# Moving two pieces of routing work on VectorE: a comparison of the third round behind two row residuals, and the one-hots of two experts ahead of the next update

## The chip, the cores and the metric

The kernel runs on one core of a Trainium2 chip. The metric is device time in microseconds (us) of one execution, as the median over executions. Engines are named as the profile names them: PE (TensorE matmul), PEld (TensorE weight load), DVE (VectorE), ACT (ScalarE), POOL (GpSimd) and SP (SyncE, which issues DMAs). POOL issues DMAs as well, the gathers and scatters by index among them.

## The reference, cut to what matters

A gated linear attention over 3072 tokens is followed by a mixture of eight experts with a hard capacity. Which expert a token gets depends on a greedy walk over all (token, expert) logits in descending order.

```python
# attention: state = alpha*state + k v^T ; y = q . state, per head -> x of shape (3072, 384)
logits = x @ w_gate                       # 3072 x 8
order = np.argsort(-logits.flatten())
for idx in order:
    tok, e = idx // E, idx % E
    if assigned[tok] >= 0 or counts[e] >= cap: continue   # cap = 384
    assigned[tok] = e; counts[e] += 1
for e in range(E):
    mask = assigned == e
    h = np.maximum(x[mask] @ w1[e], 0.0)  # 384 x 1024
    out[mask] = h @ w2[e]                 # 384 x 384
```

## The kernel before

**Two phases.** The first 135 us or so are the attention. Its engine orders come from a planner in the kernel (`Plan`), and the change doesn't touch it. The second phase routes and runs the experts, one after the other. Its order is made when the program is built. The framework takes the program order as a priority and its own estimate of durations, and fixes one order per engine, which the chip then keeps. A block under `tc.high_priority()` ranks ahead. `tc.issue_after(x)` adds an edge: the instructions of the block stand behind `x` in the order of the engine that both run on. The block waits for nothing that its data doesn't need, apart from its place in the line.

**Rounds.** Experts are handled in the order in which they fill up, so round i finds the i-th expert to be closed (i runs from 0 to 7; the third round is i = 2). Each round has these steps, all mostly on DVE with small matmuls on PE between them:

- `search(i)` (L712 on): five or six levels. A level compares a digit of each token's key with a ramp (`compare`, output `cmp`, L683), counts by matmul (`rt`, L745, L748 or L751), subtracts and compares (`need` L757 or L762, `gt` L764), sums by one matmul (L772), reduces (`k`, L776) and forms the next digit (`nd`, L779). Its end yields the expert's number (`ei`), and `weights` loads that expert's w1 and w2 in halves through SP.
- `extract(i)` (L914 on): turns the chosen tokens' ranks into a list of row numbers. It writes one-hots (`hot` L931, `rhs` L934), multiplies them on PE (`xt` L944), adds four small pieces into `idx` (L955, L956), and POOL then gathers three blocks of 128 rows of x (`xr`, L963).
- `update(i)` (L842 on): takes the closed expert out and makes the keys of round i + 1, with the first-level comparison of that round (`cmp` on a digit `dig`) in it. In the program it stands in the loop of round i + 1, ahead of `search(i + 1)`.

In rounds 0 to 2 the variable `st["hot"]` holds the last instruction of the one-hots of `extract` (the product `rhs` in rounds 1 and 2), and the next `update` is placed behind it with `issue_after`. For later rounds there is no such edge, and `update` goes where the framework puts it.

**The expert itself.** `prep(i)` (L1032 on) transposes the three gathered blocks on PE (L1046), ACT copies each as `xh` (L1049), and DVE takes the row residual `xl = xt - xh` (L1051, `XD` in the changed kernel). The transposes for expert i stand behind the matmuls of block 5 of the expert before. Then come eight blocks of `ffn1` (L1062; `hh` on ACT L1066, `hl` on DVE L1067) and `ffn2` (`y`, L1082). Every product is done as three matmuls with high and low parts. `split` makes these parts of the weights: ACT copies `w1hi`, `w1lo`, `w2hi`, `w2lo` (L1005), and a POOL DMA then adds the raw weight onto the negative copy (`w1lo`, `w2lo`, L993).

The transposes and the one-hot product share two PSUM banks (`psx`), so block 2 of the rows can be transposed only when `xl` of block 0 has been read from its bank.

The line that places the second-level comparison (`t == 1`) puts it behind the newest `idx`:

```python
            with tc.issue_after(st["idx"].ins) if i and t == 1 else ExitStack():
                nc.vector.tensor_tensor(words(dst, nt, js), keyed(d, nt, js), each(iotas[t], nt, js), op=OP.is_ge)
```

Of the kernel before, what the change touches and what calls it, by code (L numbers as in the profile page):

```python
# [157 lines left out]
def gla_moe_kernel(ctx, tc, q, k, v, alpha, w_gate, w1, w2, out):  # L158
    nc = tc.nc
# [66 lines left out]
    def each(table, n, js):  # L226
        return table[:, None, :n].to_broadcast([128, (js.stop - js.start) // U, n, U])

    def keyed(x, n, js):
        return x[:, js].rearrange("p (w u) -> p w u", u=U)[:, :, None, :].to_broadcast(  # L230
            [128, (js.stop - js.start) // U, n, U])

    def words(x, n, js):
        return x[:, js.start // U:js.stop // U, :n]
# [61 lines left out]
    def levels(i):  # L296
        return BITS if i < LATER else LATER_BITS
# [344 lines left out]
    def row(x, w=NU):  # L642
        return x[:, :, None].to_broadcast([128, NU, w])
# [32 lines left out]
    def compare(i, d, t):  # L676
        nt = 2 ** levels(i)[t]
        dst = cbuf[t % 2]
        if nt < T:
            dst = dst.rearrange("p w (h t) u -> p (w h) t u", h=T // nt)  # L680
        for js in halves(i, 2 * nt == T, 0 if t else 3):
            with tc.issue_after(st["idx"].ins) if i and t == 1 else ExitStack():
                nc.vector.tensor_tensor(words(dst, nt, js), keyed(d, nt, js), each(iotas[t], nt, js), op=OP.is_ge)  # L683
            yield dst, js

    def halves(i, pairs, parts=0):
        if i == 1 and not pairs and parts:
            return [slice(a, a + NU // parts) for a in range(0, NU, NU // parts)]
        if i:
            return [slice(0, NU)]  # L690
        return [slice(0, 16), slice(16, NU)] if pairs else [slice(0, NU // 2), slice(NU // 2, NU)]
# [4 lines left out]
    def pair(x, j):  # L696
        return x.rearrange("p w t u -> p (w t u)")[:, 64 * U * (j // U) + j % U:64 * U * (j // U + 2):U]

    st = dict(chu=chu0, o=o0, dig=dig0)

    def spin_after(n, *after):
        if n:
            o = fps.tile([128, CAP], F32, name="h", bufs=2)
            with ExitStack() as es_:
                for x in after:
                    es_.enter_context(tc.issue_after(x.ins))
                for _ in range(n):
                    x = nc.tensor.matmul(o, warm[:, :128], warm[:, :CAP], start=True, stop=True)
            after = [x]
        return after  # L710

    def search(i):  # L712
# [12 lines left out]
        for t, bits in enumerate(levels(i)):  # L725
# [3 lines left out]
            else:  # L729
                g = (gs if i < LATER else later_gs[bits])[t % 2]  # L730
                parts = compare(i, d, t) if t else [(cbuf[0], js) for js in halves(i, False)]
                rt = fps.tile([128, 64], F32, name="rt")
                two, four = 2 * nt == T, 4 * nt == T
# [180 lines left out]
    def extract(i):  # L914
        vi = rw.tile([128, NU], I16, name="vi")
        if st["v1"] is None:
            nc.vector.tensor_scalar(vi, st["v"], -1.0, None, op0=OP.add)
        else:
            nc.vector.scalar_tensor_tensor(vi, st["v"], -1.0, st["v1"], op0=OP.add, op1=OP.add)
        wi = rw.tile([128, NU], I16, name="wi")  # L920
        nc.vector.tensor_scalar(wi, vi, 63, None, op0=OP.bitwise_and)
        bi = rw.tile([128, NU], I16, name="bi")
        nc.vector.tensor_scalar(bi, vi, 32704, None, op0=OP.bitwise_and)
        bk = rw.tile([128, NU, 2 * NB], F16, name="bk")
        x = nc.vector.tensor_tensor(bk, row(bi, 2 * NB), bsel, op=OP.is_equal)
        hot = rw.tile([128, NW, 64, U], F16, name="hot", bufs=1)
        rhs = rw.tile([128, NU, 2 * NB], F16, name="rhs")
        alone = i == 0
        for a, js in enumerate(halves(i, True)):
            with tc.issue_after(x.ins):  # L930
                x = nc.vector.tensor_tensor(words(hot, 64, js), keyed(wi, 64, js), each(iota_0, 64, js), op=OP.is_equal)  # L931
            if a == 0:
                with tc.issue_after(x.ins):
                    y = nc.vector.tensor_tensor(rhs, bk, cst, op=OP.mult)  # L934
                x = y
        if i < 3:
            st["hot"] = x
        ix = psx.tile([128, 2, 2, NB], F32, name="xt")
        with ExitStack() as es_:
            if i == 0:  # L940
                for x in st["spin"]:
                    es_.enter_context(tc.issue_after(x.ins))
            for j in [j for j in range(NU) if j // U % 2 == 0]:
                st["picked"] = nc.tensor.matmul(ix, pair(hot, j), rhs[:, j:j + U + 1:U],  # L944
                                                start=(j == 0), stop=(j == NU - U - 1))
        IDX[i] = rw.tile([128, NB], I32, name="idx", bufs=4)
        lo, hi = slice(0, 64), slice(64, 128)
        other = rw.tile([128, NB], F32, name="other")
        if alone:
            nc.scalar.activation(other[hi], ix[lo, 0, 1], AF.Copy)  # L950
            nc.vector.tensor_copy(other[lo], ix[hi, 1, 0])
        else:
            nc.vector.tensor_copy(other[lo], ix[hi, 1, 0])
            nc.vector.tensor_copy(other[hi], ix[lo, 0, 1])
        nc.vector.scalar_tensor_tensor(IDX[i][lo], ix[lo, 0, 0], float(N // 2), other[lo], op0=OP.add, op1=OP.add)  # L955
        st["idx"] = nc.vector.scalar_tensor_tensor(IDX[i][hi], ix[hi, 1, 1], float(N // 2), other[hi],  # L956
                                                   op0=OP.add, op1=OP.add)
        if i == 0:
            st["spin"] = spin_after(WARM_IN_ROUTE[0], st["picked"])
        if i:  # L960
            XR[i] = wp.tile([128, NB, Dm], F32, name="xr")
        for b in range(NB):
            gathers[b] = last_gather[0] = nc.gpsimd.indirect_dma_start(  # L963
                out=XR[i][:, b], out_offset=None, in_=x_dram,
                in_offset=bass.IndirectOffsetOnAxis(ap=IDX[i][:, b:b + 1], axis=0))

        for load_, b in second_half:
            tc.add_manual_dep(load_(1).ins, gathers[b].ins.name,
                              mybir.DependencyInfo(mybir.DependencyClass.Sync, mybir.DependencyReason.DATA),
                              reason="rows of the first experts before their later weights")  # L970
        second_half.clear()

    last_gather, gathers = [None], {}

    XH, XL, CH, XA = {}, {}, {}, {}

    def split(i, hf):
        fs = slice(hf * F // 2, (hf + 1) * F // 2)
# [53 lines left out]
    def prep(i):  # L1032
        hi = wp.tile([128, DB, CAP], F32R, name="xh")
        lo = fp.tile([128, DB, CAP], F32R, name="xl")
        for b in range(NB):
            bs = slice(b * 128, (b + 1) * 128)
            o = psx.tile([128, DB, 128], F32, name="xt")
            with ExitStack() as es:
                if i:
                    es.enter_context(tc.issue_after(F2[i - 1, FB - 3].ins))  # L1040
                else:
                    st["spin"] = spin_after(WARM_IN_ROUTE[1 + b], *st["spin"])
                    for x in st["spin"]:
                        es.enter_context(tc.issue_after(x.ins))
                for d in range(DB):
                    x = nc.tensor.transpose(o[:, d], XR[i][:, b, d * 128:(d + 1) * 128], ident)  # L1046
                if i == 0:
                    st["spin"] = [x]
            XA[i] = nc.scalar.activation(hi[:, :, bs], o, AF.Copy)  # L1049
            with tc.high_priority():  # L1050
                nc.vector.tensor_sub(lo[:, :, bs], o, hi[:, :, bs])  # L1051
        XH[i], XL[i] = hi, lo

    HH, HA, F1, HL = {}, {}, {}, {}
# [47 lines left out]
    for n in range(E * FB + 2):  # L1102
        i, q = divmod(n, FB)
# [17 lines left out]
        if n >= 2:  # L1121
            i, q = divmod(n - 2, FB)
# [53 lines left out]
```

## Time and profile before

| | |
|---|---|
| median of 3 executions | 416.37 us (413.94, 416.37, 419.88) |
| the profiled execution's own time | 413.29 us |
| its span, from the first to the last instruction | 411.6 us |
| PE busy over the span | 385.0 us (94%) |
| PEld busy | 340.6 us (83%) |
| DVE busy | 283.3 us (69%) |
| ACT busy | 214.5 us (52%) |
| POOL busy | 186.8 us (45%) |
| mean granted TensorE clock | 0.991 |

The profile is of one execution. A row of the order of time gives the start in us, the duration in us, the engine, the line of the kernel, the operation, what it writes and reads with the shapes, and in square brackets how long the engine had been idle just before and what ended that idle time. Durations overlap a little with the next row on the same engine, so the spacing of starts is the better measure of what one instruction costs. Everything between the last instruction and the end of the execution (413.29 less 411.6, 1.69 us) lies outside the span.

### The profile page before, as it was taken

Reading aid. Unit: us, or ns where it says so; the run is one execution under the profiler, and the core shown is the slowest. Engines: PE = TensorE matmul, PEld = TensorE weight load, DVE = VectorE, ACT = ScalarE, POOL = GpSimd, SP = SyncE. Lnnn points to the kernel's source line nnn. Section 1 sums busy time; section 2 is a strip of 40 time slices with the busy share of each in tenths; the row PEclk is TensorE's granted clock in tenths of the full one; section 3 lists DMA queues with packets and bytes.
Section 4 is the critical chain, followed back from the end, with each engine's and each line's share of the span. In section 5 each row is a group of like instructions: output and inputs, shape, how many; then the busy total and the mean of one; then the engine's idle time right before and its main releaser. Section 6 shows DMA issues by size and latency. Waiting matters only on the chain.

```text
span 411.6 us, 9897 instructions
## 1 busy us (share of the span) xinstructions
PE 385.0 (94%) x3775; PEld 340.6 (83%) x3775; DVE 283.3 (69%) x909; ACT 214.5 (52%) x382; POOL 186.8 (45%) x230
## 2 busy tenths in 40 slices
PE   6899999999999888898999998999999999999992
PEld 3788889887888556797798997899998999999992
DVE  8889997899994686687586796597796872312210
ACT  3456555654553015626639629529529539478211
POOL 5899988566851016213405506216126263614102
PEclk9899999999999999999999999999999999999998
DMA  8989898763020148789799999979999999999601
GB/s 274 378 284 309 276 311 230 245 200 105 22 79 30 50 151 204 164 204 262 206 220 323 200 282 274 213 252 278 210 298 226 197 303 327 247 305 202 155 0 58
DMA packets 43711, 88.05 MB, mean 214 GB/s; under 512 B 3856, under 2 KB 18192, under 8 KB 43664
## 3 DMA queue, kind: packets, MB, share of 16 engines
q0 software_dynamic: 11408, 33.83, 38.9%
q1 hardware_dynamic: 32256, 53.60, 38.5%
q8 instruction: 29, 0.48, 0.5%
q14 instruction: 18, 0.15, 0.1%
HBM read 53.59 MB, written 9.44 MB: 153 GB/s over the span
## 4 chain that ended last, share of the span: by engine, by line
PE 48%; DVE 16%; issue 15%; DMA 14%; POOL 3%; ACT 1%; POOLq 0%; SPq 0%; DVEq 0%
PE h L1062 12%; PE y L1082 11%; DMA w1r<-in_moe_w_dram 4%; PE xt L421 4%; PE y L484 4%; DMA w1lo<-w1r 4%; PE y L477 4%; PE s L433 4%; DMA xr<-x_dram,idx 3%; DMA w2lo<-w2r 3%; DVE te L393 3%; PE lg L502 2%; DVE tp L399 2%; PE rt L751 1%; PE st L445 1%
## 5 line engine op out<-in xcount | busy, mean ns | idle before, releaser
L1066 ACT ACTIVATE hh<-h 128x384 fp32r<-128x384 f32 x64 | 31.3, 488 | 85.3 <-PE h L1062 62.5
L1067 DVE SCALAR_TENSOR_TENSOR hl<-h,hh 128x384 fp32r<-128x384 f32 x64 | 35.4, 553 | 51.0 <-ACT hh L1066 50.7
L1082 PE MATMUL y<-w2hi,hh 128*128 128x384 f32 x192 | 66.6, 347 | 0.0
L1082 PE MATMUL y<-w2lo,hh 128*128 128x384 f32 x192 | 65.8, 343 | 0.4 <-DMA w2lo<-w2r 0.4
L1082 PE MATMUL y<-w2hi,hl 128*128 128x384 f32 x192 | 65.3, 342 | 0.0
L1094 POOL DMA_INDIRECT out_dram<-yt,idx x24 | 25.5, 1062 | 50.5 <-ACT yt L1087 46.8
L1062 PE MATMUL h<-xh,w1lo 128*128 128x384 f32 x192 | 46.9, 343 | 0.0
L1062 PE MATMUL h<-xh,w1hi 128*128 128x384 f32 x192 | 46.0, 342 | 0.6 <-ACT xh L1049 0.6
L1062 PE MATMUL h<-xl,w1hi 128*128 128x384 f32 x192 | 45.8, 342 | 0.0
L993 POOL DMA_DIRECT2D w1lo<-w1r x15 | 20.3, 1350 | 55.7 <-ACT w1lo L1005 40.1
L963 POOL DMA_INDIRECT xr<-x_dram,idx x24 | 26.2, 1092 | 40.4 <-DVE idx L956 26.2
L1062 PEld LDWEIGHTS h<-xh,w1hi 128*128 128x128 f32 x192 | 33.9, 188 | 4.4 <-issue 2.9
L403 POOL TENSOR_TENSOR kh<-rk,te 128x512 f32<-128x512 f32 (+1 forms) x24 | 29.4, 1226 | 17.1 <-DVE z L413 11.4
L1082 PEld LDWEIGHTS y<-w2lo,hh 128*128 128x128 f32 x192 | 36.3, 189 | 0.7 <-DMA w2lo<-w2r 0.7
L1082 PEld LDWEIGHTS y<-w2hi,hh 128*128 128x128 f32 x192 | 36.3, 189 | 0.0
L1082 PEld LDWEIGHTS y<-w2hi,hl 128*128 128x128 f32 x192 | 36.2, 189 | 0.1
L1062 PEld LDWEIGHTS h<-xl,w1hi 128*128 128x128 f32 x192 | 33.8, 189 | 0.5 <-DVE xl L1051 0.2
L1062 PEld LDWEIGHTS h<-xh,w1lo 128*128 128x128 f32 x192 | 33.9, 189 | 0.4 <-DMA w1lo<-w1r 0.3
L1005 ACT ACTIVATE w1hi<-w1r 128x768 fp32r<-128x768 f32 x32 | 26.8, 840 | 10.4 <-DMA w1r<-in_moe_w_dram 8.0
L435 ACT ACTIVATE sm<-s 128x1024 f32<-128x1024 f32 x24 | 24.6, 1026 | 13.9 <-PE s L433 13.4
L399 DVE TENSOR_TENSOR_SCAN tp<-al,z 128x512 f32<-128x512 f32 (+1 forms) x26 | 29.6, 1138 | 2.6 <-DVE z L413 0.5
L393 DVE TENSOR_TENSOR_SCAN te<-al,z 128x511 f32<-128x511 f32 (+2 forms) x26 | 30.8, 1186 | 0.5
(204 smaller groups left out, 833.8 us busy)
## 6 DMA issues: line engine op xcount, KB each, us to landing
w1r<-in_moe_w_dram SPq DMA_DIRECT2D x16, 768.0 KB, 7.7
w2r<-in_moe_w_dram SPq DMA_DIRECT2D x16, 768.0 KB, 10.0
w2lo<-w2r POOLq DMA_DIRECT2D x16, 768.0 KB, 10.4
w1lo<-w1r POOLq DMA_DIRECT2D x15, 768.0 KB, 8.0
al<-in_alpha_dram SPq DMA_DIRECT2D x24, 260.0 KB, 4.1
rk<-in_k_dram SPq DMA_DIRECT2D x24, 256.0 KB, 4.2
rq<-in_q_dram SPq DMA_DIRECT2D x24, 256.0 KB, 4.4
rv<-in_v_dram SPq DMA_DIRECT2D x24, 192.0 KB, 3.9
```

The costliest lines, as they stand in the source:

```text
L393: nc.vector.tensor_tensor_scan(te.t[:, lo:top][:, ::-1], al.t[:, lo + 1:top + 1][:, ::-1], zb[:, lo + 1:top + 1][:, ::-1], al.t[:, 4 * C + ...
L399: nc.vector.tensor_tensor_scan(tp.t[:, lo:hi], al.t[:, lo:hi], zb[:, lo:hi], 1.0, op0=OP.mult, op1=OP.add)
L403: eng.tensor_tensor(out_.t[:, us].rearrange("p u c -> p (u c)"), x.t[:, lo:hi], f.t[:, lo:hi], op=OP.mult)
L435: add(A_, 1.05, lambda: nc.scalar.activation(sm.t, sc.t, AF.Copy), r=[(sc, 0), (sc, 1)], w=[sm])
L963: gathers[b] = last_gather[0] = nc.gpsimd.indirect_dma_start(out=XR[i][:, b], out_offset=None, in_=x_dram, in_offset=bass.IndirectOffsetOn ...
L993: return nc.gpsimd.dma_start(x.bitcast(F32), raw_, accum_op=OP.add, max_dma_last_dim=8192)
L1005: nc.scalar.activation(dst, src, AF.Copy, scale=scale)
L1062: F1[i, q] = nc.tensor.matmul(o, a[:, d], x[:, d], start=(n == 0), stop=(n == 3 * DB - 1))
L1066: HA[i, q] = nc.scalar.activation(hh, o, AF.Relu)
L1067: HL[i, q] = nc.vector.scalar_tensor_tensor(hl, o, 0.0, hh, op0=OP.max, op1=OP.subtract)
L1082: F2[i, q] = nc.tensor.matmul(Y[b], a[:, bs], w, start=(q == 0 and n == 0), stop=(q == FB - 1 and n == 2))
L1094: st_ = nc.gpsimd.indirect_dma_start(out=out, out_offset=bass.IndirectOffsetOnAxis(ap=IDX[i][:, b:b + 1], axis=0), in_=yt, in_offset=None)
```

## The change

Two orders on DVE are written anew; no instruction is added or taken out.

1. In round 2 the second-level comparison stands behind `XD[1, 1]`, the row residual of the second block of expert 1 (and so behind that of the first block too), where it stood behind `idx` of round 1. All other rounds keep their place for it.
2. `st["hot"]` is kept for rounds 0 to 4, where it was kept for rounds 0 to 2. So `update(3)` and `update(4)` stand behind the one-hots of `extract(3)` and `extract(4)`, the fourth and fifth expert.

```diff
@@ compare
-            with tc.issue_after(st["idx"].ins) if i and t == 1 else ExitStack():
+            behind = XD[1, 1] if i == 2 else st.get("idx")
+            with tc.issue_after(behind.ins) if i and t == 1 else ExitStack():
@@ extract
-        if i < 3:
+        if i < 5:
             st["hot"] = x
@@
-    XH, XL, CH, XA = {}, {}, {}, {}
+    XH, XL, CH, XA, XD = {}, {}, {}, {}, {}
@@ prep
             with tc.high_priority():
-                nc.vector.tensor_sub(lo[:, :, bs], o, hi[:, :, bs])
+                XD[i, b] = nc.vector.tensor_sub(lo[:, :, bs], o, hi[:, :, bs])
```

## The prediction, made before the changed kernel ran

> **What bounds the kernel now.** First the page's head, then busy time in stretches of the expert phase, then PE's waits from 180 us to the end.
>
> ```profile
> span 411.6 us, 9897 instructions
> PE 385.0 (94%) x3775; PEld 340.6 (83%) x3775; DVE 283.3 (69%) x909; ACT 214.5 (52%) x382; POOL 186.8 (45%) x230
> 176.00:210.00 34.00, 31.60 (x257) 28.44 (x256) 24.35 (x90) 18.07 (x30) 10.73 (x10) 1.00 0.91 225
> 210.00:240.00 30.00, 29.12 (x224) 26.88 (x223) 23.13 (x95) 18.14 (x30) 11.30 (x10) 1.00 1.04 255
> 240.00:262.00 22.00, 19.94 (x157) 17.76 (x156) 15.83 (x64) 14.79 (x24) 7.61 (x7) 1.00 1.02 270
> 262.00:300.00 38.00, 37.98 (x287) 34.61 (x286) 29.62 (x128) 21.22 (x37) 13.13 (x14) 1.00 0.98 239
> 300.00:340.00 40.00, 40.00 (x295) 37.09 (x294) 30.94 (x134) 21.93 (x36) 16.61 (x14) 1.00 0.99 260
> ```
>
> The stretch rows give the stretch, its length, then busy time of PE, PEld, DVE, ACT and POOL, the granted clock, the DMA share and GB/s. From 262 us on PE is never free (37.98 of 38, 40.00 of 40), at a clock of 1.00. So PE's work sets the end, and what the change can take out is PE's idle time ahead of 262 us: 34.00 - 31.60 = 2.40, then 0.88, then 2.06, together 5.34 us. Both edits act after 190 us. PE's waits say who caused it (total, times, longest; the first two):
>
> ```profile
> PE xt L1046 <- DMA xr<-x_dram,idx: 3.0, 2, 1.6
> PE rt L772 <- DVE gt L764: 1.3, 2, 0.9
> ...
> ```
>
> More than half is waiting for gathered rows. One of these two waits (3.0 - 1.6 = 1.4 us, expert 1) lies ahead of both edits. The other is expert 3's, and the order of time shows it with the rest of what can move:
>
> ```profile
> 196.99 0.98 PE L1062 MATMUL h<-xh,w1hi 128*128 128x384 f32 x4 [0.57 <-ACT xh L1049]
> ...
> 201.66 0.44 PE L1082 MATMUL y<-w2lo,hh 128*128 128x384 f32 x1 [0.42 <-DMA w2lo<-w2r]
> ...
> 221.11 0.17 PE L772 MATMUL rt<-gt,one 128*128 128x8 bf16 x1 [0.88 <-DVE gt L764]
> ...
> 252.65 0.17 PE L772 MATMUL rt<-gt,one 128*128 128x8 bf16 x1 [0.42 <-DVE gt L764]
> ...
> 257.90 1.02 PE L1046 MATMUL xt<-ident,xr 128*128 128x128 f32 x6 [1.64 <-DMA xr<-x_dram,idx]
> ```
>
> **The change, edit 2 first (one-hots of experts 3 and 4 ahead of the update).** DVE and POOL in round 3:
>
> ```profile
> 241.02 0.25 DVE L837 SCALAR_TENSOR_TENSOR v<-cum,rt,qe 128x24 f32<-128x24 f32 x1
> ...
> 244.03 0.95 DVE L683 TENSOR_TENSOR cmp<-dig,iota 128x1536 bf16<-128x1536 bf16 x1
> ...
> 246.68 0.94 DVE L931 TENSOR_TENSOR hot<-wi,iota 128x1536 f16<-128x1536 int16 x1
> ...
> 249.26 0.17 DVE L956 SCALAR_TENSOR_TENSOR idx<-xt,other 64x3 int32<-64x3 f32 x1
> 249.46 0.96 DVE L683 TENSOR_TENSOR cmp<-nd,iota 128x1536 bf16<-128x1536 bf16 x1
> ...
> 249.34 1.33 POOL L993 DMA_DIRECT2D w1lo<-w1r  x1 [13.84 <-ACT w1lo L1005]
> 250.98 1.07 POOL L963 DMA_INDIRECT xr<-x_dram,idx  x1 [0.30 <-issue]
> ```
>
> The whole update ran between v and hot, and on POOL a w1lo DMA stood in front, so the gather began 250.98 - 241.02 = 10.0 us after v. Rounds 1 and 2 already have the new order:
>
> ```profile
> 179.22 0.25 DVE L837 SCALAR_TENSOR_TENSOR v<-cum,rt,qe 128x24 f32<-128x24 f32 x1 [0.30 <-PE rt L830]
> ...
> 183.13 1.09 POOL L963 DMA_INDIRECT xr<-x_dram,idx  x1 [8.11 <-DVE idx L956]
> ...
> 211.12 0.25 DVE L837 SCALAR_TENSOR_TENSOR v<-cum,rt,qe 128x24 f32<-128x24 f32 x1
> ...
> 217.73 1.65 POOL L963 DMA_INDIRECT xr<-x_dram,idx  x1 [10.34 <-DVE idx L956]
> ```
>
> There the gather began 3.9 and 6.6 us after v. Expert 3's will therefore begin between 241.02 + 3.9 = 244.9 and 241.02 + 6.6 = 247.6, ahead of the w1lo DMA of 249.34, which is 3.4 to 6.1 us earlier than before. The rows should arrive as much earlier, and the 1.64 us wait goes even at the lesser end. What stands late next is PE itself: the transposes keep their place behind block 5 of expert 2, whose matmuls ended at 257.90 - 1.64 = 256.26. **Term A: -1.64 us.** For expert 4 the same is worth nothing on PE, because 262 to 300 has no idle time; PE's own work hides it.
>
> The price of edit 2 is that update(3) and update(4), and with each the first comparison of the next round, start later by the extract instructions put ahead:
>
> ```profile
> 213.64 0.16 DVE L844 SCALAR_TENSOR_TENSOR pen<-cl,pen 128x8 f32<-128x8 f32 x1
> ...
> 221.80 0.96 DVE L683 TENSOR_TENSOR cmp<-nd,iota 128x1536 bf16<-128x1536 bf16 x1
> ...
> 224.74 0.56 DVE L683 TENSOR_TENSOR cmp<-nd,iota 128x768 bf16<-128x768 bf16 x1
> ```
>
> In round 2, 213.64 - 211.12 = 2.52 us passed from v to pen, the update's first instruction. An hl between them (0.47 by spacing, as xl of the same size below) and the two v (0.25 to 0.5) come off: 1.7 us. So the first comparison of round 4 moves from 244.03 to about 245.7. Before, 5.43 us passed from it to the second one (249.46), because that stood behind idx and the extract instructions sat between its steps. A level without them takes 224.74 - 221.80 = 2.94 us. With the four pieces of idx (0.2 each, by 249.26 to 249.46) and an hl (0.47) it is 4.2, and the second comparison comes at 249.9 against 249.46; without these it would be 248.6. I take 0 for the later rounds, between -0.8 and +0.4; if the planned order leaves the steps as far apart as they are, it is +1.7.
>
> **Edit 1 (the comparison of round 2 behind two residuals).**
>
> ```profile
> 191.94 0.49 ACT L1049 ACTIVATE xh<-xt 128x384 fp32r<-128x384 f32 x1 [0.66 <-PE xt L1046]
> ...
> 192.99 1.76 DVE L683 TENSOR_TENSOR cmp<-nd,iota 128x3072 bf16<-128x3072 bf16 x1
> 194.66 1.01 DVE L1051 TENSOR_TENSOR xl<-xt,xh 128x384 fp32r<-128x384 f32 x2
> ...
> 196.97 0.56 DVE L1051 TENSOR_TENSOR xl<-xt,xh 128x384 fp32r<-128x384 f32 x1 [0.32 <-ACT xh L1049]
> 197.44 0.23 DVE L779 SCALAR_TENSOR_TENSOR nd<-nd,k,dig 128x24 bf16<-128x24 bf16 x1
> ```
>
> Both inputs of the two residuals were there at 192.43, but they waited for a comparison of 1.7 us, and block 2's transposes, xh and the first matmul of expert 1 waited with them. Turned round, the residuals end about 1.7 us earlier, and the comparison starts 1.0 us later (two residuals), or 0.5 if the first of them fits into the wait for k. Queued behind the comparison are that level's count, k and nd, and then all of round 2 up to the weights of expert 2. In return the third residual (0.47 us, with 0.32 of waiting) no longer stands in front of the next nd, which gives 0.8 back: the search comes out between -0.3 and +0.2. On PE the 0.57 at 196.99 can go, but PE then meets the w2lo DMA earlier, which ends at 201.6 whatever DVE does, so its 0.42 grows to 1.0. **Term B: 0**, between -0.6 (if PE has other work for that wait) and +1.0 (if nothing is given back: weights of expert 2 later, ACT's copies later, and the 0.88 at 221.11 longer). The 0.42 at 252.65 lies in DVE's reordered stretch and can go or double; I take 0 and keep both ends.
>
> Sum: 413.29 - 1.64 = 411.65 us for an execution like the profiled one (span 411.6 - 1.64 = 409.96; the 1.69 us outside it stay). That execution was faster than all three timed ones, so on the median 416.37 - 1.64 = **414.7 us**, with -0.6 to -2.6 of change (413.8 to 415.8) as this case's own range.
>
> **Rivals.** *The earlier gather takes its time from the weights.* The four weight halves of expert 3 are in flight then:
>
> ```profile
> 240.67 0.38 SPq L658 DMA_DIRECT2D w1r<-in_moe_w_dram  x1
> ...
> GB/s 221 180 229 179 229 125 305 317 384 368 399 405 399 394 380 379 352 164 172 188 183 188 120 219 349 378 211 242 188 213 188 191 205 199 202 240 188 248 188 205
> ...
> 251.65 0.56 DVE L1067 SCALAR_TENSOR_TENSOR hl<-h,hh 128x384 fp32r<-128x384 f32 x1 [1.23 <-ACT hh L1066]
> ...
> 252.25 0.83 ACT L1005 ACTIVATE w1hi<-w1r 128x768 fp32r<-128x768 f32 x1
> ```
>
> The second row cuts 238 to 268 us into 40 slices. While the loads ran alone they moved 380 to 405 GB/s (about 245 to 250 us). The gather's three blocks (3 x 128 x 384 x 4 bytes, 0.59 MB) are 1.5 us at 394 GB/s. ACT copies these weights, and hh stands between the copies: hl waited 1.23 us for it, and the 0.42 at 252.65 is gt behind that hl. Loads 1.5 us late would cost PE 1.5 there: -1.64 + 1.5, **416.2 us**. [...] The trace of before has no gather beside loads at full rate, so it can't settle this. Against it: the copy of the second half of w1 began at 252.25 without a wait, so ACT was behind the loads already.
>
> *The pushed updates carry through (the other side).* If the 1.7 us of rounds 4 and 5 stay, the weights of experts 4 and 5 come 1.7 and 3.4 us later, while PE is 1.64 earlier. Their slack shows in the landing of the first w2lo:
>
> ```profile
> 285.02 1.03 POOL L993 DMA_DIRECT2D w2lo<-w2r  x1
> ...
> w2lo<-w2r POOLq DMA_DIRECT2D x1, 768.0 KB, 9.1
> ...
> 295.83 0.34 PE L1082 MATMUL y<-w2lo,hh 128*128 128x384 f32 x1
> ```
>
> Issued at 285.02, it landed at 294.1, 1.7 us before its use. It decides from a delay of 0.1 us on, once PE is 1.64 earlier: expert 4 gives back 1.6, expert 5 another 1.7. Net -1.64 + 3.3 = +1.7: **418.1 us**. Against it: expert 4's w2lo stood behind its gathers on POOL, and these come earlier too.
>
> *The waits of DVE's order go as well.* If also 0.57, 0.42 and the 0.88 of 221.11 vanish, it is -1.64 - 1.87 = -3.5: **412.9 us**. For it speaks that a DVE order caused them; against it the w2lo landing.
>
> *The order doesn't change.* Excluded: cmp at 192.99 precedes xl at 194.66, and the update's comparison at 244.03 precedes hot at 246.68.
>
> **How the numbers follow.** Chances: forecast 0.50, gather against weights 0.20, pushed updates 0.15, more waits gone 0.12, others 0.03. The range must hold all but the outermost: from 412.9 less 1.1 to the 418.1 of the slower rival, the more so because the three executions of before differ by 6 us: 411.8 to 418.2. About 2% is what a measurement of this kernel tells from no change, and that is 8.3 us. Even all 5.34 us of idle time are less, so faster by 2% gets 0.02; slower by 2% gets 0.03, for an order that leaves PE without work in several rounds; within 2% gets 0.95.
>
> **What would show it.** In the changed profile: idx of round 3 before 247.5 and its gather ahead of the w1lo DMA; no PE wait for xr at expert 3, and PE at its transposes at 256.3; the second comparison of round 4 at 249 to 250; in round 2 xl, xl, then cmp, with PE's wait for w2lo near 1.0 and none for xh. The forecast is wrong if PE's wait turns up at 252 (weights), at the first w2lo of experts 4 and 5 (updates), or grows beyond 0.88 at 221.

## The result, and the profile after

The change made the kernel slower by 0.8%: 418.60 us (median of 20 executions) against 415.46 us (20), ratio 1.0077 with a 95% interval of 1.0048 to 1.0107. The forecast was 414.7 us, within 411.8 to 418.2. The sign was wrong, and the median lies just above the range. The forecast stood on the 416.37 of three executions; from 415.46 the same sum gives 413.8. All ratios here and below are of the fast executions alone, those within 1.5% of their kernel's fastest, so they are not the quotients of the medians beside them.

The profiled execution of the changed kernel took 420.92 us. Line numbers stand one higher than before from `compare` on. First the head of its page:

```profile
span 418.9 us, 9895 instructions
...
PE 390.0 (93%) x3775; PEld 344.6 (82%) x3775; DVE 285.2 (68%) x909; ACT 214.3 (51%) x382; POOL 187.2 (45%) x230
```

Then its busy time in the stretches shown of before (PE, PEld, DVE, ACT, POOL, clock, DMA share, GB/s):

```profile
176.00:210.00 34.00, 32.58 (x264) 29.29 (x263) 23.51 (x81) 17.35 (x29) 11.93 (x11) 0.95 0.87 218
210.00:240.00 30.00, 29.47 (x224) 26.98 (x224) 22.39 (x93) 18.64 (x31) 11.36 (x10) 1.00 1.03 252
240.00:262.00 22.00, 18.20 (x141) 16.61 (x141) 14.62 (x64) 10.79 (x17) 6.04 (x5) 1.00 0.96 262
262.00:300.00 38.00, 38.00 (x279) 34.73 (x278) 27.70 (x113) 24.12 (x40) 15.23 (x14) 0.96 0.87 213
300.00:340.00 40.00, 38.37 (x282) 35.11 (x282) 31.35 (x142) 20.18 (x34) 11.80 (x11) 1.00 1.01 244
```

Up to 240 us PE did lose less: 34.00 - 32.58 = 1.42 and 0.53 us idle, against 2.40 and 0.88. Then it lost more: 3.80 us against 2.06 between 240 and 262, and 1.63 against 0.00 between 300 and 340. PE's instructions also took longer, 390.0 us against 385.0 for the same 3775, and the clock says why (0.95 and 0.96 in two stretches, and a fall ahead of them, below). PE's waits from 176 us on, in order of time:

```profile
191.64 0.55 PE L1047 MATMUL xt<-ident,xr 128*128 128x128 f32 x3 [1.38 <-DMA xr<-x_dram,idx]
222.47 0.17 PE L773 MATMUL rt<-gt,one 128*128 128x8 bf16 x1 [0.39 <-DVE gt L765]
260.65 0.55 PE L1047 MATMUL xt<-ident,xr 128*128 128x128 f32 x3 [3.67 <-DMA xr<-x_dram,idx]
319.12 0.17 PE L773 MATMUL rt<-gt,one 128*128 128x8 bf16 x1 [1.41 <-DVE gt L765]
...
370.21 0.81 PE L1063 MATMUL h<-xh,w1lo 128*128 128x384 f32 x3 [0.67 <-DMA w1lo<-w1r]
```

The 0.57, 0.42 and 0.42 of before are gone and the 0.88 is 0.39. The wait for expert 3's rows, which the forecast took away, has grown from 1.64 to 3.67 us. DVE and POOL in round 3 show why the rows weren't earlier:

```profile
243.68 0.25 DVE L838 SCALAR_TENSOR_TENSOR v<-cum,rt,qe 128x24 f32<-128x24 f32 x1 [0.20 <-PE rt L831]
...
245.18 0.95 DVE L932 TENSOR_TENSOR hot<-wi,iota 128x1536 f16<-128x1536 int16 x1
...
249.39 0.96 DVE L684 TENSOR_TENSOR cmp<-dig,iota 128x1536 bf16<-128x1536 bf16 x1
...
250.71 0.16 DVE L957 SCALAR_TENSOR_TENSOR idx<-xt,other 64x3 int32<-64x3 f32 x1
253.59 0.96 DVE L684 TENSOR_TENSOR cmp<-nd,iota 128x1536 bf16<-128x1536 bf16 x1
...
252.12 1.34 POOL L994 DMA_DIRECT2D w1lo<-w1r  x1 [15.40 <-ACT w1lo L1006]
253.75 1.74 POOL L964 DMA_INDIRECT xr<-x_dram,idx  x1 [0.30 <-DVE nd L780]
```

The one-hots do stand ahead of the update now, and `idx` ended 250.87 - 243.68 = 7.2 us after v instead of 8.4. But POOL still had the `w1lo` DMA in front of the gather, and that DMA waits for ACT's copies. So the gather began 2.9 us after `idx` was done, and 253.75 - 243.68 = 10.07 us after v, against 9.96 before. PE, relieved of small waits, came to its transposes 260.65 - 3.67 - 243.68 = 13.30 us after v, against 256.26 - 241.02 = 15.24 before. The arithmetic closes: 1.64 + (15.24 - 13.30) + (10.07 - 9.96) = 3.69. **Counted from v, all that PE had saved was handed back at this wait**, because the gather's time behind v didn't move with it.

Two things came on top. First, the clock behind the long wait, in the changed kernel:

```profile
262.00:265.00 3.00, 3.00 (x14) 2.60 (x12) 1.30 (x5) 2.45 (x4) 1.31 (x1) 0.53 0.66 133
265.00:268.00 3.00, 3.00 (x24) 2.83 (x22) 2.07 (x8) 1.98 (x4) 1.05 (x1) 0.91 0.93 161
```

PE was busy all the time and got 0.53 and 0.91 of its clock: 3 x 0.47 + 3 x 0.09 = 1.7 us lost. Before, behind a wait of 1.64, it was 1.00. Second, the 1.41 at 319.12, which ACT and DVE explain:

```profile
313.93 0.84 ACT L1006 ACTIVATE w1hi<-w1r 128x768 fp32r<-128x768 f32 x1 [3.36 <-DMA w1r<-in_moe_w_dram]
...
317.62 0.47 ACT L1067 ACTIVATE hh<-h 128x384 fp32r<-128x384 f32 x1
318.12 0.56 DVE L1068 SCALAR_TENSOR_TENSOR hl<-h,hh 128x384 fp32r<-128x384 f32 x1 [1.88 <-ACT hh L1067]
318.91 0.16 DVE L765 TENSOR_TENSOR gt<-rt,need 64x8 bf16<-64x8 f32 x1
```

ACT stood 3.36 us for a weight load, with five copies ahead of `hh` in its queue. DVE's `hl` waited for `hh`, and the search's `gt` stood behind `hl`.

From 176 us on PE idled 7.74 us, the rows above and one of 0.22, against 5.29 before: +2.45, and 1.7 by the clock at 262 to 268. The two profiled executions differ by 7.6 us, the medians by 3.1. So this execution also holds losses that others don't. The clock fell twice ahead of all this: to 0.76 and 0.67 in the 3 us from 165 and from 168, and to 0.81 and 0.62 in those from 192 and from 195, where the kernel before had 1.00. That is 3 x (0.24 + 0.33 + 0.19 + 0.38) = 3.4 us, the larger part of PE's 5.0. The waits in front (1.29 us at 165.17, 1.38 at 191.64) come ahead of both edits, and e20 below, which has neither edit, shows 0.86 and 0.57, and 0.91 and 0.52, in the same stretches. So these 3.4 us are not the edits'.

### The profile page after: what moved, and what is told of

The parts are those of the page before. It is cut to its first block, busy times and chain, and to the rows that moved or that the text cites. A ratio compares the mean times of both kernels' runs of the same rounds, so it can differ in the third digit from the quotient of the medians.

```text
span 418.9 us, 9895 instructions
## 1 busy us (share of the span) xinstructions
PE 390.0 (93%) x3775; PEld 344.6 (82%) x3775; DVE 285.2 (68%) x909; ACT 214.3 (51%) x382; POOL 187.2 (45%) x230
## 4 chain that ended last, share of the span: by engine, by line
PE 45%; issue 18%; DVE 16%; DMA 14%; POOL 4%; ACT 2%; POOLq 0%; DVEq 0%; SPq 0%; ACTq 0%
PE y L1083 10%; PE h L1063 9%; DMA xr<-x_dram,idx 5%; PE xt L421 4%; DMA w1lo<-w1r 4%; PE y L484 4%; PE s L433 4%; PE y L477 4%; DMA w1r<-in_moe_w_dram 3%; DVE te L393 3%; PE lg L502 2%; DVE tp L399 2%; DMA out_dram<-yt,idx 2%; PE xt L1047 2%; PE h L709 2%
## 5 line engine op out<-in xcount | busy, mean ns | idle before, releaser
L1083 PE MATMUL y<-w2hi,hh 128*128 128x384 f32 x192 | 67.7, 353 | 0.0
L1083 PE MATMUL y<-w2lo,hh 128*128 128x384 f32 x192 | 67.3, 351 | 0.0
L1083 PE MATMUL y<-w2hi,hl 128*128 128x384 f32 x192 | 66.3, 347 | 0.0
```

Source lines behind the costliest of these rows:

```text
L1083: F2[i, q] = nc.tensor.matmul(Y[b], a[:, bs], w, start=(q == 0 and n == 0), stop=(q == FB - 1 and n == 2))
```

## The experiments

Theory 1: the gather behind `w1lo` on POOL makes the loss. Theory 2: the pushed updates of rounds 4 and 5 make it. Theory 3: the longer wait's clock. All ratios are against executions of the kernel before that were timed with the run, with a 95% interval. The median of these was 414.4 to 415.5, so ratios are better compared than medians.

**Each edit alone.** e1 keeps edit 1 only:

```diff
-        if i < 5:
+        if i < 3:
             st["hot"] = x
```

> Edit 1 alone (comparison of round 2 behind the residuals; the one-hots of experts 3 and 4 as before). Theory A (the later comparison delays rounds 2 and 3, and with them the weights and the gather of expert 3, which stands behind the w1lo DMA on POOL): PE's wait for xr at expert 3 is above 2.5 us, and the time is 1.5 to 3.5 us above the kernel before. Theory B (the pushed updates of rounds 3 and 4 are to blame): the wait stays near 1.6 us or below, and the time is within 1 us of before or less. Theory C (no order is to blame, the changed kernel's orders only fall worse with the transfers of expert 0): within 1 us of before.

Measured: 416.56 us, 1.0062 (1.0023 to 1.0102). PE and POOL of e1 in order of time:

```profile
256.95 1.02 PE L1047 MATMUL xt<-ident,xr 128*128 128x128 f32 x6 [2.96 <-DMA xr<-x_dram,idx]
...
248.40 1.34 POOL L994 DMA_DIRECT2D w1lo<-w1r  x1 [14.85 <-PE xt L945]
250.04 1.07 POOL L964 DMA_INDIRECT xr<-x_dram,idx  x1 [0.30 <-DVE cmp L684]
```

Its busy time and clock just behind the wait:

```profile
259.00:262.00 3.00, 3.00 (x19) 2.60 (x19) 0.89 (x2) 2.19 (x4) 1.30 (x1) 0.51 0.60 114
```

Edit 1 does speed PE up: its idle time from 176 to 240 is 1.39 us in e1, 3.23 before. PE came to the transposes at 253.99, found no rows, waited 2.96, and got half its clock for 3 us. It waited another 1.44 us for the rows of expert 4, at 291.06. The saving turned into longer waits, and the clock's 1.5 us added to the loss. The expectation of e1 had put such a wait down to later routing, but v of round 3 came 240.49 - 190.40 = 50.09 us after expert 1's transposes began, and 241.02 - 190.20 = 50.82 before. PE was early, and the routing wasn't late.

e2 keeps edit 2 only (`compare` as before); e3 and e4 take it apart by expert:

```diff
-        if i < 3:
+        if i < 4:             # e3: expert 3 alone
+        if i < 3 or i == 4:   # e4: expert 4 alone
             st["hot"] = x
```

> Edit 2 alone, both experts. Theory A: within 1 us of the kernel before, with PE's wait for xr at expert 3 at 0.5 to 2 us. Theory B: 2 to 4 us slower, with a new wait at expert 4 or 5 (around 319 us in the changed kernel, 1.4 us, for gt). Theory C: within 1 us. The prediction on record would have 1.6 us faster, with no wait for xr at expert 3.

> Edit 2 for expert 3 alone (update(3) behind its one-hots, update(4) as before, edit 1 left out). Theory A: within 1 us of before. Theory B: if the push of round 4 is the loss, 1 to 2 us slower; if it is that of round 5, none. On POOL the gather of expert 3 stands behind the w1lo DMA as before, so it begins no more than 1 us earlier than 250.98, and PE's wait for xr stays between 0.6 and 1.7 us.

> Edit 2 for expert 4 alone (update(4) behind its one-hots, update(3) as before, edit 1 left out). Theory A: within 1 us of before, PE's wait for xr at expert 3 unchanged (1.6 us). Theory B with round 5 as the place: 1 to 3 us slower, with a new wait of PE after 300 us.

Measured: e2 417.26, 1.0058 (1.0019 to 1.0098); e3 418.63, 1.0104 (1.0045 to 1.0162; six executions); e4 414.44, 0.9998 (0.9961 to 1.0034). In e2 PE waited 2.50 us for expert 3's rows. The same wait in e3, where 0.6 to 1.7 was expected, in order of time:

```profile
260.75 0.48 PE L1046 MATMUL xt<-ident,xr 128*128 128x128 f32 x1 [2.54 <-DMA xr<-x_dram,idx]
```

The clock in e3 behind it:

```profile
262.00:265.00 3.00, 3.00 (x13) 2.84 (x12) 1.81 (x5) 2.13 (x4) 0.42 (x1) 0.50 1.04 194
```

And the wait in e4:

```profile
258.38 0.55 PE L1046 MATMUL xt<-ident,xr 128*128 128x128 f32 x3 [1.01 <-DMA xr<-x_dram,idx]
```

So the part that moves expert 3's one-hots, the one the forecast's gain came from, costs by itself, and its mark is the wait it should have removed. Its gather began 9.83 (e2) and 9.50 us (e3) after v, hardly earlier than the 9.96 of before, and the transposes could start 17.50 and 17.22 us after v, against 16.88. Why the rows took longer there isn't settled. Nor is all of e3's loss the edit's: its profile also has the clock at 0.50 in 192 to 195 and at 0.61 in 222 to 225, ahead of what the edit moves. Expert 4's part costs nothing.

**The gathers put first on POOL.** e5 is the changed kernel with one edge more, e6 the kernel before with the same edge, e13 edit 1 alone with it:

```diff
@@ split, low()
-                if i == 0 or i < 3 and not hf:
+                if i == 0 or i < 4 and not hf:
                     es.enter_context(tc.issue_after(last_gather[0].ins))
```

> The changed kernel, with one more edge on POOL: the first w1lo DMA of expert 3 stands behind expert 3's gathers (as those of experts 1 and 2 do already). Theory D (expert 3's gather waits for the w1lo in front of it on POOL, not for idx, so the earlier idx buys nothing; the longer wait of PE then also lowers its clock): the gather begins about 0.3 us after idx, some 2.5 us earlier relative to the rest; PE's wait for xr at expert 3 falls from 3.7 to 1.5 us or less, the granted clock behind it stays at 1.00, and the time falls by 2.5 to 4.5 us from the changed kernel, to 414 to 416. Theory E (the loss is the pushed updates of rounds 3 and 4 or chance): within 1 us of the changed kernel, 417.5 to 419.5.

> The kernel before, with the same edge on POOL alone (first w1lo of expert 3 behind its gathers). Theory D: the gather begins at about 249.7 where it began at 250.98, PE's wait for xr at expert 3 falls from 1.6 to about 0.3 us, and the time falls by 0.5 to 1.5 us. Theory E: no change.

> Edit 1 alone with the edge on POOL (first w1lo of expert 3 behind its gathers). Theory D: in the run with edit 1 alone PE came to expert 3's transposes 2.3 us earlier than before and waited 3.0 us for rows whose gather began 1.3 us after idx; with the gather first the wait is 1.5 to 2.2 us, the clock mostly stays, and the time is 1 to 2.5 us below that run, 414 to 415.6. Theory E: within 1 us of edit 1 alone (416.6).

Measured: e5 415.38, 1.0013 (0.9984 to 1.0042): the loss is gone. But e6 took 417.01, 1.0058 (1.0028 to 1.0088), and e13 419.72, 1.0133 (1.0097 to 1.017; six executions): without the change's second edit the same edge made the kernel slower, against what both expectations said. In none of the three does PE wait for expert 3's rows. Each has a new wait at about 284, shown here for e5 (PE, ACT and DVE in order of time):

```profile
283.69 0.17 PE L773 MATMUL rt<-gt,one 128*128 128x8 bf16 x1 [1.99 <-DVE gt L765]
...
280.29 0.85 ACT L1006 ACTIVATE w1hi<-w1r 128x768 fp32r<-128x768 f32 x1 [4.86 <-DMA w1r<-in_moe_w_dram]
...
282.51 0.47 ACT L1067 ACTIVATE hh<-h 128x384 fp32r<-128x384 f32 x1
...
283.01 0.56 DVE L1068 SCALAR_TENSOR_TENSOR hl<-h,hh 128x384 fp32r<-128x384 f32 x1 [2.41 <-ACT hh L1067]
283.49 0.15 DVE L765 TENSOR_TENSOR gt<-rt,need 64x8 bf16<-64x8 f32 x1
```

The same for e6 (PE and ACT):

```profile
284.83 0.17 PE L772 MATMUL rt<-gt,one 128*128 128x8 bf16 x1 [2.43 <-DVE gt L764]
...
279.64 0.85 ACT L1005 ACTIVATE w1hi<-w1r 128x768 fp32r<-128x768 f32 x1 [4.40 <-DMA w1r<-in_moe_w_dram]
...
283.33 0.47 ACT L1066 ACTIVATE hh<-h 128x384 fp32r<-128x384 f32 x1
```

It is the chain of 319 in the changed kernel: ACT's copies for expert 4 have their place ahead of `hh` and wait there for a load that the routing issues late. With one wait taken from PE (3.67 us in the changed kernel, 1.64 before), it ran into the next queue whose order was fixed for a slower PE (1.99 us in e5, 2.43 in e6).

**ACT's copies one place later as well.** e14 is e5, e15 is e6, each with this edit. e23 and e20 have it without the edge on POOL, on the changed kernel and on the kernel before:

```diff
@@ split, behind()
-            return HA[i - 1, SPLIT_AFTER[i > 1]] if i and not hf else None
+            return HA[i - 1, SPLIT_AFTER[i > 1] + (i == 4)] if i and not hf else None
```

> This is e5 (the change, with the first w1lo of expert 3 behind its gathers) and one edit more: ScalarE's weight copies of expert 4 stand behind the sixth activation of expert 3 (hh of chunk 5) and not behind the fifth. In e5 they stood ahead of the sixth, waited there 4.86 us for their w1r (to 280.29), held the finished h back (hh 282.51, and behind it hl 283.01 and gt 283.49 on VectorE), and TensorE waited 1.99 us for gt at 283.69. Theory A (the time that the routing gives back is lost where a copy that waits for a late load holds up hh on ScalarE): the wait at 283.7 goes to under 0.5, no new wait over 0.7 before 300, the clock stays 1.00, time about 413.4 (2.0 under e5's 415.4). Theory B (TensorE runs up against the routing of the next round wherever it is freed): as much as is taken away there comes back as a wait for xr, gt or w1lo by 300, time 415.0 to 415.8. Rival C (the planner sets the other engines anew and that alone decides): over 416.

> This is e6 (the kernel before, with the first w1lo of expert 3 behind its gathers) and the same edit of ScalarE's order for expert 4. In e6 the copies waited 4.40 us for w1r (to 279.64), hh came at 283.33, and TensorE waited 2.43 us for gt at 284.83, and then 0.93 for xr at 294.17. Theory A: the wait of 2.43 goes, time 417.0 less 2.4, 414.6; and if so, the change's own edits are worth 414.6 less e14. Theory B: waits of the same sum come by 300 (xr of expert 4 above all), 416.5 to 417.5. Rival C: what the other engines' new order gives, either way by over 1.

> The change with ScalarE's weight copies of expert 4 behind the sixth activation of expert 3, as in e14, and without e14's edge on GpSimd: the plan still has the first w1lo of expert 3 ahead of its gathers. If the gathers behind that w1lo are what made the change slower, TensorE waits 2.5 to 3.7 us for xr at about 260 and its clock falls to 0.5 to 0.7 for some 3 us behind it, as in the changed kernel, and the time is 416.5 to 418.5: ScalarE's order alone brings at most the difference of small waits. If the copies on ScalarE were the cause in the changed kernel too, it comes near to e14's 412.8, under 414.5.

> The kernel before with ScalarE's copies of expert 4 behind the sixth activation of expert 3, and nothing else. The kernel before had no wait over 0.7 us between 262 and 330, so this edit has nothing to take away: 414.6 with 413.8 to 415.4, and the wait of 1.64 for xr at 257.9 stays. If it gains by over 1 us, ScalarE's order is worth something by itself, and e14's and e15's times are to be read less that.

The eight kernels together, with their ratios:

| | as it was | ACT later | gathers first | both |
|---|---|---|---|---|
| without the change | 415.46 | 415.61, 1.0011 (0.9973 to 1.0049) | 417.01, 1.0058 (1.0028 to 1.0088) | 414.40, 1.0023 (0.9994 to 1.0053) |
| with the change | 418.60, 1.0077 (1.0048 to 1.0107) | 419.21, 1.0090 (1.0055 to 1.0124) | 415.38, 1.0013 (0.9984 to 1.0042) | 412.81, 0.9981 (0.9946 to 1.0016) |

e14 and e15 came out as the theory of ACT's order said (413.4 and 414.6 expected). e23 has the wait and the clock that the theory of the gather said, and its 419.21 lies above the 416.5 to 418.5 expected. e20, at 415.61, lies just above its 413.8 to 415.4 and shows no gain. ACT, PE, DVE and POOL of e14:

```profile
278.50 0.49 ACT L1067 ACTIVATE hh<-h 128x384 fp32r<-128x384 f32 x1 [3.14 <-PE h L1063]
280.06 0.85 ACT L1006 ACTIVATE w1hi<-w1r 128x768 fp32r<-128x768 f32 x1 [1.07 <-DMA w1r<-in_moe_w_dram]
...
285.25 0.17 PE L773 MATMUL rt<-gt,one 128*128 128x8 bf16 x1 [0.37 <-DVE gt L765]
...
244.20 0.25 DVE L838 SCALAR_TENSOR_TENSOR v<-cum,rt,qe 128x24 f32<-128x24 f32 x1 [0.20 <-PE rt L831]
...
251.66 1.02 POOL L964 DMA_INDIRECT xr<-x_dram,idx  x1 [14.41 <-DVE idx L957]
```

PE and POOL of e23:

```profile
258.26 0.55 PE L1047 MATMUL xt<-ident,xr 128*128 128x128 f32 x3 [3.44 <-DMA xr<-x_dram,idx]
...
249.97 1.34 POOL L994 DMA_DIRECT2D w1lo<-w1r  x1 [15.72 <-ACT w1lo L1006]
251.60 1.73 POOL L964 DMA_INDIRECT xr<-x_dram,idx  x1 [0.30 <-DVE nd L780]
```

The clock of e23 behind the wait:

```profile
259.00:262.00 3.00, 3.00 (x21) 2.90 (x18) 1.57 (x6) 2.29 (x4) 0.65 (x1) 0.56 0.97 197
```

In e14 the copies begin at the same time, but `hh` is done ahead of them, and the 1.99 of e5 is 0.37. In e23 ACT's order alone leaves the wait for rows (3.44) and the clock's fall (0.56) where they were, and the loss too. So in the changed kernel the place of the `w1lo` DMA makes the loss. What ACT's order brings once that is mended is 2.6 us by the medians with the change and without it (415.38 to 412.81, 417.01 to 414.40); the intervals of each pair overlap, and it is the waits that show it.

e14 has the lowest median of all, but its interval holds no change, so it isn't shown to beat the kernel before. Against the changed kernel it is faster: the two intervals don't meet. e17 put the first `w1lo` of every expert behind its gathers, with ACT as in e14. e16 did that too and moved ACT's copies for experts 3 to 7:

> As e14, and the first w1lo of every expert is behind its gathers (in e14 that of expert 5 stands ahead of them by the plan). Theory A: as e14 to 300, and at expert 5 (about 320) no wait for xr where e14 may have one; 413.0 to 413.4. Theory B: 415.0 to 415.8. If e17 and e14 agree to 0.5, the order on GpSimd at expert 5 matters nothing, and the wait at expert 3 was the one that cost.

> The change, with the first w1lo of every expert behind its gathers and ScalarE's copies of experts 3 to 7 behind the sixth activation of the expert before. Theory A: no wait of hh behind a copy that waits for w1r, none for xr; but copies that begin 3.3 us later leave w1lo later, so a wait for w1lo or w2lo of 0.5 to 2 per expert is possible where the load was in time (experts 5 to 7, whose w1r came before hh in e5: 340.26, 367.20): 413 to 416. Theory B: 415 to 416. Rival: weights late at experts 5 to 7, 418 to 422.

Measured: e17 414.47, 1.0015 (0.9985 to 1.0046), and e16 413.34, 0.9991 (0.9962 to 1.002). The forecast for e17 failed: 413.0 to 413.4 was expected if ACT's order were all. PE of e17:

```profile
348.52 0.55 PE L1047 MATMUL xt<-ident,xr 128*128 128x128 f32 x3 [1.83 <-DVE xl L1052]
```

PE of e16:

```profile
349.73 0.44 PE L1063 MATMUL h<-xh,w1lo 128*128 128x384 f32 x1 [1.93 <-DMA w1lo<-w1r]
```

e16 has no wait between 219 and 349 us, and both give nearly 2 us back at expert 6. e16's is the late `w1lo` that its rival named. The intervals of e14, e16 and e17 overlap, so no order among them is shown.

**The clock by itself.** e11 is the changed kernel with 12 idle matmuls ahead of expert 3's transposes, so that PE works while it waits:

```diff
@@ prep
                 if i:
                     es.enter_context(tc.issue_after(F2[i - 1, FB - 3].ins))
+                    if i == 3 and b == 0:
+                        for x in spin_after(12, F2[i - 1, FB - 3]):
+                            es.enter_context(tc.issue_after(x.ins))
```

> The changed kernel with 12 matmuls on a constant (2.1 us of PE work whose result is not used) in front of expert 3's transposes, where PE waits for the gathered rows. It measures the clock's part by itself. Theory D: the wait of 3.7 us shrinks by about the filler, rows arrive as before, the granted clock in the 6 us behind it stays above 0.95 where it was 0.53 and 0.91, and the time falls by 1 to 2 us from the changed kernel. If the clock's fall has no part in the loss, the time stays within 0.5 us of the changed kernel or rises.

Measured: 415.53, 1.0038 (1.0007 to 1.0069). Its row for the wait:

```profile
259.36 0.55 PE L1050 MATMUL xt<-ident,xr 128*128 128x128 f32 x3 [0.70 <-DMA xr<-x_dram,idx]
```

Its clock behind it:

```profile
262.00:265.00 3.00, 3.00 (x19) 2.77 (x19) 2.28 (x8) 1.63 (x4) 1.29 (x2) 1.00 1.03 196
```

The clock stays at 1.00, and about half of the loss goes (1.0077 to 1.0038, 1.6 us of 3.2), near the 1.5 to 1.7 that the clock's rows give. The intervals of the two overlap, and the filler also changed the planned order on POOL for expert 5, so this is support, not proof.

Each execution's mean granted clock is on record too, and the part missing to 1, times the span, is an estimate of what the clock took from it. Means over all executions: 4.3 us in the kernel before (116 executions), 6.4 in the changed kernel (20), 4.7 in e11, 4.2 in e5 and 4.3 in e14. So some 2 of the 3.2 us go with the clock, and most of them come back in e11 and all of them where the gathers stand first with the change.

## Why the prediction was wrong, point by point

- **What bounds the kernel**: right that PE's work and idle time set the end, wrong that its instructions keep their length. PE's busy time rose by 5.0 us for the same count, but 3.4 of them lie ahead of the edits; 1.7 lie behind the longer wait.
- **Term A (-1.64), the step that failed.** "Expert 3's will therefore begin between ... 244.9 and ... 247.6, ahead of the w1lo DMA of 249.34". It took rounds 1 and 2 as the model for round 3. But in `low()` the first `w1lo` of experts 0 to 2 is placed behind the gathers by an edge (`i < 3 and not hf`), and expert 3's isn't. The plan put it in front, before and after the change. Also the new first comparison (249.39) kept its place ahead of `idx`, where in round 2 `idx` comes first. So `idx` began 250.71 - 243.68 = 7.0 us after v, against 8.2 before, and not 6.2 (217.29 - 211.12) or less as in the model rounds. Where the gathers stood first (e14), they began 251.66 - 244.20 = 7.46 us after v: 2.5 us gained, less than the 3.4 to 6.1 foretold, but enough: PE's wait went. It also went in e6, e13 and e15, which lack edit 2 and have the gather 8.7 us after v. So the `w1lo` DMA in front held the rows up, and moving the one-hots was not needed to end the wait.
- **The price of edit 2 (0, between -0.8 and +0.4; +1.7 if the steps stay apart), mis-sized.** The steps did move together: 253.59 - 249.39 = 4.20 us, the 4.2 foretold, against 5.43 before. But the first comparison came 249.39 - 243.68 = 5.7 us after v, against 3.0, and so moved by 2.7 and not by 1.7. The prediction took an `hl` and the two v off the 2.52 us from v to `pen`. They stayed: `pen` came at 246.20, 2.52 after v, and before it had stood at 240.89, ahead of v. So the second comparison came 9.9 us after v, against 8.4: +1.5, outside the stated ends and near the slower rival's 1.7, though not by its condition.
- **Term B (0, -0.6 to +1.0), mis-sized.** Its order came as foretold (`xl` twice, then `cmp`):

```profile
194.31 1.01 DVE L1052 TENSOR_TENSOR xl<-xt,xh 128x384 fp32r<-128x384 f32 x2
195.24 1.75 DVE L684 TENSOR_TENSOR cmp<-nd,iota 128x3072 bf16<-128x3072 bf16 x1
```

  The wait for xh went, but the `w2lo` wait of 0.42 didn't grow to 1.0, it went as well: 1.5 us less idle from 176 to 240 (3.23 to 1.77), 1.8 in e1, where the clock stayed at 1.00 there. Treated as hidden, it was the very thing that made PE early for rows which weren't.
- **The rivals.** *Gather against weights*: not seen; no gather came ahead of the loads, and no run shows loads that end later by a gather's 1.5 us: that was the author's estimate. *Pushed updates* (418.1): the nearest in time, and its push of 1.5 us happened, but e4 (expert 4 alone) costs nothing, and e5 and e14, which keep both pushes, don't lose. Its price wasn't what was paid. *More waits gone* (412.9): they did go, and this was half right: with both queues mended (e14) the time is 412.81. That the two numbers agree is luck, since e14 has two edges that the rival hadn't.
- **What wasn't reckoned**: that behind a longer wait PE's clock fell as well (0.53 in the 3 us behind 3.67 us; 1.00 behind the 1.64 of before). This is about half of the loss by e11; the clock as a whole, wherever it fell, is some two thirds by the estimate over all executions.
- With both orders mended, with and without the change (e14, e15), it is 412.81 against 414.40, -1.6 us, the size of term A. Their intervals overlap, so that this gain is the edits' is indicated, not shown.

Left open: e13, at 419.72 worse than e6 with a chain like e6's. Its own 2.44 us wait at 283.58 was followed by a clock of 0.51 and 0.50 over 6 us, which e6's wasn't, and it has a wait of 1.03 us for `w1lo` at 261.00, 0.15 in e6. But its profile is of the fastest of the six executions (416.92), so it can't show all that the median paid. By the mean clock, e13's executions lost 6.8 us and e6's 6.0, against 4.3 before (an estimate as above); the rest of e13's loss is not settled. Also open: four of the nine profiles with edit 1 (e5, e11, e13, e23) have a wait of 1.1 us for `gt` in round 2, at 197 to 200 us, with the clock at 0.50 behind it, and none of the seven without edit 1 has it.

## What to carry to other kernels

An instruction that starts earlier because its input is ready earlier must still get past what stands ahead of it in its own engine's queue (here the gather began 2.9 us after its `idx`, with the `w1lo` DMA in front): read that queue for the same round, and the edges that put it in order, before taking another round as the model. When PE is freed of a wait, list for each later queue (gathers on POOL, copies on ACT) how long it was ahead of PE; the saving ends at the first that was not ahead by as much (in e5 and e6 the copies on ACT, at 1.99 and 2.43 us). Count a long PE wait at more than its length where the clock falls behind it (in the changed kernel 1.7 us more behind those of 1.29, 1.38 and 3.67 us, none behind that of 1.41), and mend the order that causes it before removing the smaller waits in front of it.

## What the runs showed of the hardware

**The granted clock fell behind some waits shorter than 3 us and not behind others.** Two stretches of 3 us behind a wait of 2.44 us in e13:

```profile
283.00:286.00 3.00, 2.42 (x19) 2.11 (x20) 1.15 (x5) 3.00 (x6) 2.39 (x3) 0.51 0.71 131
286.00:289.00 3.00, 3.00 (x13) 2.69 (x12) 1.04 (x3) 2.16 (x3) 2.70 (x4) 0.50 1.09 182
```

One behind the wait of 2.43 us in e6:

```profile
287.00:290.00 3.00, 2.76 (x20) 2.38 (x19) 2.16 (x8) 3.00 (x6) 2.40 (x4) 1.00 1.07 191
```

The waits of 2.50 to 3.67 us for expert 3's rows all cost it (0.50 to 0.63 in the lowest stretch of 3 us), those of 1.64 and less there didn't. But expert 1's wait of 1.35 us in e14 was followed by 0.50, and before's 1.36 by 1.00. Nor did the length decide: 1.93 us in e16 was followed by 0.54, and 1.99 in e5 by 1.00. The price of a fall was steady: in steps of 1 us, of the 22 falls between 150 and 404 us in the sixteen profiles 20 lost 1.70 or 1.71 us each, and two lost twice that (3.41 in e13, 3.42 in e3). In the changed kernel the three falls have their lowest steps at 0.50, in 167 to 170, 194 to 197 and 263 to 265. What decides whether a fall follows a wait, these runs don't show.

**A small DVE instruction ended when POOL's arithmetic did.** `nd` in round 0 of the changed kernel, with POOL's four subtractions:

```profile
161.57 1.76 DVE L780 SCALAR_TENSOR_TENSOR nd<-dig,k 128x24 bf16<-128x24 bf16 x1
...
158.99 4.29 POOL L1024 TENSOR_TENSOR w1lo<-w1r,w1hi 128x384 fp32r<-128x384 f32 x4
```

`nd` ended at 163.33, when POOL did (163.28), and took 1.76 us. In the kernel before it took 0.41 there, and in later rounds, where POOL does no arithmetic, 0.23 to 0.25. In all sixteen profiles the end of `nd` in round 0 lies 0.04 to 0.06 us behind POOL's, at lengths of 0.41 to 1.93. It began at 161.57, and at 161.63 before, so its length follows POOL's end. POOL began at 158.99, and at 157.74 before: the `w2lo` DMA in front stood 1.70 us, and 0.49 before, for ACT's `w2lo`, which had waited 1.59 us, and 0.26 before, for the load of `w2r`. So this is one of the losses that one execution has and another hasn't. That POOL holds `nd` up is the author's reading of the common end; no run takes POOL's subtractions away.

**POOL's gathers took longer beside a long DVE comparison.** In the sixteen profiles are 384 gathers of rows. The 196 that run beside no `cmp` and no `hot` took 0.95 to 1.09 us. Of the 90 that run beside one for over 0.5 us, 76 took over 1.25, up to 1.77; why 14 did not is open. The changed kernel's first gather for expert 3 (253.75, 1.74 us, beside the `cmp` of 253.59) is one of them; before, it took 1.07.
